# Seven products instead of eight in the second network's first layer, over 576 tokens

## The chip, the cores and the metric

The kernel runs on one core of a Trainium2 chip. The metric is the device time of one launch in microseconds (us). Between runs the time moves by about 0.2%. The core's engines run side by side, each through its own list of instructions in order: TensorE (PE; its weight loads are PEld), VectorE (DVE), ScalarE (ACT), GpSimd (POOL), and SyncE (SP), whose list holds the DMAs.

## What is computed

An attention of 4 batches, 8 heads, 576 tokens and 64 dimensions, in two parts that are added: a softmax in a window of 3 tokens to either side, and one over queries, keys and values averaged four by four. Its 2304 x 512 result goes through two networks:

```python
    a = x @ w_a            # 512 -> 1536
    b = x @ w_b
    x = a * b @ w_out      # 1536 -> 512
    h = x @ w_in           # 512 -> 2048
    g = np.maximum(h, 0.0) + alpha * np.minimum(h, 0.0)
    return (g @ w_out2)    # 2048 -> 512
```

The weights come as 64-bit floats.

## The kernel before

A matrix product in nearly fp32 is made of three fp16 ones: each operand is split into a high and a low half (`split`: ScalarE writes the scaled high half, VectorE the rest), and high x high, high x low and low x high are summed in one PSUM bank. Weights are first narrowed from 64 to 32 bits (`narrow`, three VectorE instructions), then scaled by a power of two found from the sum of their squares (`top_of`: a small fp32 transpose and matmul on TensorE between VectorE steps), then split.

The first network takes 288 tokens at a time (block j of 8): `s1(j, f)` makes 24 matmuls for one of 12 slices of hidden units and multiplies the two results, `s2(j, d)` makes 36 for one of 4 slices of the result, and `x2_out` scales, splits and writes it to DRAM. The second network takes 384 tokens at a time (6 blocks): `s3(j, f)` makes 12 matmuls of 384 columns for each of 16 slices of 128 hidden units, ScalarE takes the two halves of the leaky Relu out of the bank, VectorE joins them and the result is split into `g3`; `s4(j, t)` makes 48 matmuls of 512 columns for one of 3 tiles of 128 tokens, ScalarE scales the tile and a DMA writes it. `wi_chunk` prepares w_in, `wo2_words`, `wo2_fac` and `split_rows` prepare w_out of the second network.

No loop is issued as written. Each piece is put on a nominal time (`on`), in which order the instructions are recorded; a planner finds what each must wait for by the memory it touches, and puts every engine's list in order by a cost for each instruction (`cost`), the longest way to the end and a table of biases by name (`URGENT`). The matmuls of s1 to s4 are kept in the order of their nominal times (`chain`). `FILLS` puts matmuls of a constant tile ahead of given TensorE pieces. Since all calls go through the planner, the profile shows one line, L269, for all of them, and instructions are told apart by the tiles: `wab` and `wo` are the weights of the first network, `xt` its input, `zone` a large area that holds the attention's data first and the second network's weights later, `m`, `a` and `r` are PSUM banks (four, three and one), `tm` small buffers, `x2s` and `gt` results.

## Time and profile before

| | us |
|---|---|
| median of 3 runs (lowest, highest) | 994.26 (993.77, 995.93) |
| the profiled execution, and its span | 995.89, 994.2 |
| TensorE, VectorE, ScalarE busy in the span | 972.6, 582.8, 461.7 |
| 1152 matmuls of s3, 864 of s4, busy | 188.2, 187.6 |

The profile follows one execution. In the table a busy time is the time in which an engine had something running; matmuls overlap, so what a stream of them costs is read from the start of one group to the start of the next. The head, the first 130 us or so, holds the loads, the attention of the first batch and the first weights; then the first network runs with the other batches' attention between its matmuls, and from 615.96 us the second network.

### The profile page before, as it was taken

What the parts mean: (1) busy time and instruction counts of PE and PEld (TensorE: products, weight loads), DVE (VectorE), ACT (ScalarE), POOL (GpSimd) and SP (SyncE); (2) the same over time, 40 slices, a digit from 0 to 9 for tenths busy, and PEclk for the clock granted to TensorE, in tenths of its full rate; (3) what the DMA queues carried; (4) which work ended last, traced back from release to release, by engine and by line L of the source; (5) the groups of instructions that cost most, each with busy time, mean ns of one, the idle gap of its engine ahead of it and who ended that gap; (6) DMA issues with size and microseconds to landing.
All of it is one profiled execution on the core that took longest, in us unless ns stands there. A gap on an engine that the chain in (4) does not pass through costs nothing.

```text
span 994.2 us, 18276 instructions
## 1 busy us (share of the span) xinstructions
PE 972.6 (98%) x7443; PEld 668.4 (67%) x7443; DVE 582.8 (59%) x1270; ACT 461.7 (46%) x1123; POOL 41.1 (4%) x84
## 2 busy tenths in 40 slices
...
PEclk9998999999999999999999999999999999999999
...
GB/s 187 236 281 145 182 87 1 26 78 85 50 2 52 110 47 72 86 109 64 189 131 170 4 19 31 1 53 12 32 32 1 54 35 32 32 1 17 17 1 32
DMA packets 95940, 69.47 MB, mean 70 GB/s; under 512 B 71152, under 2 KB 78704, under 8 KB 95856
## 3 DMA queue, kind: packets, MB, share of 16 engines
...
## 4 chain that ended last, share of the span: by engine, by line
PE 88%; DVE 8%; DMA 1%; SPq 1%; ACT 1%; issue 1%; ACTq 0%
PE m L269 77%; PE a L269 9%; DVE wab L269 2%; DVE zone L269 2%; DVE wo L269 1%; PE r L269 1%; SPq L269 1%; DMA wo<-in_moe_w_b_dram 1%; DVE xt L269 1%; DMA gt<-in_v_dram 1%; DVE nm L269 1%; ACT zone L269 0%; DVE tm L269 0%; DVE gt L269 0%; DVE nz L269 0%
## 5 line engine op out<-in xcount | busy, mean ns | idle before, releaser
L269 PEld LDWEIGHTS <-wab 128*128 128x128 f16 x3168 | 306.6, 98 | 160.3 <-issue 4.1
L269 PE MATMUL m<-xt,wab 128*128 128x288 f16 x2304 | 296.0, 286 | 2.0 <-DVE xt L269 1.5
L269 PE MATMUL m<-xt,zone 128*128 128x384 f16 x1152 | 188.2, 326 | 0.0
L269 PE MATMUL m<-zone,wab 128*128 128x512 f16 x864 | 187.6, 379 | 0.0
L269 PEld LDWEIGHTS <-zone 128*128 128x128 f16 x1152 | 112.6, 98 | 74.7
L269 DVE SCALAR_TENSOR_TENSOR gt<-tm,nal,tm 128x384 f32<-128x384 f32 x96 | 59.4, 619 | 137.9 <-ACT tm L269 126.6
L269 PEld LDWEIGHTS <-wo 128*128 128x128 f16 x1152 | 111.4, 98 | 28.4 <-issue 0.6
L269 ACT ACTIVATE tm<-m 128x384 f32<-128x384 f32 (+1 forms) x224 | 95.0, 467 | 58.7 <-PE m L269 55.1
L269 PE MATMUL m<-gt,wo 128*128 128x288 f16 x864 | 109.5, 286 | 0.0
L269 DVE SCALAR_TENSOR_TENSOR wab<-gt,kap,wab 128x384 f16<-128x384 f32 x96 | 59.3, 618 | 56.6 <-ACT wab L269 56.6
L269 ACT ACTIVATE gt<-m,uf 128x512 f32<-128x512 f32 x18 | 12.4, 687 | 161.4 <-PE m L269 161.4
L269 ACT ACTIVATE wab<-gt,kap 128x384 f16<-128x384 f32 x96 | 59.0, 615 | 56.5 <-DVE gt L269 56.5
L269 PE MATMUL a<-zone 64*96 64x104 f32 (+4 forms) x1046 | 70.2, 266 | 0.0
L269 PEld LDWEIGHTS a<-zone 64*96 64x96 f32 (+4 forms) x1046 | 56.5, 149 | 18.8 <-issue 15.5
L269 ACT COPY zone<-a 104x384 f32<-104x384 f32 (+4 forms) x119 | 50.6, 470 | 31.7 <-PE a L269 31.4
L269 ACT ACTIVATE zone<-zone 128x512 bf16<-128x512 f32 (+4 forms) x48 | 39.0, 812 | 46.1 <-DVE zone L269 37.2
L269 ACT ACTIVATE gt<-tm 128x288 f16<-128x288 f32 x72 | 31.9, 442 | 51.8 <-DVE tm L269 51.4
L269 ACT COPY tm<-m 128x288 f32<-128x288 f32 x96 | 37.7, 395 | 34.5 <-PE m L269 34.2
L269 DVE SCALAR_TENSOR_TENSOR tm<-m,tm 128x288 f32<-128x288 f32 x96 | 42.7, 447 | 18.7 <-PE m L269 15.9
L269 PE MATMUL a<-idf,zone 96*104 96x96 f32 (+4 forms) x384 | 40.6, 248 | 4.3 <-DVE zone L269 4.3
L269 POOL TENSOR_TENSOR zone<-zone 72x256 f32<-72x256 f32 x36 | 32.2, 908 | 301.0 <-DMA zone<-in_v_dram 223.6
L269 DVE TENSOR_REDUCE zone<-zone 128x96 f32<-128x384 f32 x48 | 24.9, 545 | 32.6 <-ACT zone L269 32.5
...
## 6 DMA issues: line engine op xcount, KB each, us to landing
...
```

The lines of the kernel that those rows point to most:

```text
L269: f(*args, **kw)
```

## The change

Strassen's scheme in Winograd's form makes a product of 2 x 2 blocks from seven block products and fifteen additions. Here the blocks are two halves of the 512 inputs, two slices of 128 hidden units and two halves of 576 tokens. `wi_chunk` makes the seven operands of the weights (three blocks and four sums) in fp32 before the split, `x2_prep` those of the input, for which x2 is now kept in DRAM as fp32. A quarter, `s3(j, q)`, makes 14 products (`prod`, 6 matmuls of 288 columns each) for two chunks of weights side by side; each half r owns three banks (`sb3`), and sums that are needed twice stay in a bank after a copy. `done` forms the leaky Relu as max(-h, 0) x (1 - alpha) + h. The second network has 4 blocks of 576 tokens; s4 has 4 or 5 tiles after each, 18 in all. The seven operands need more room: the second network's output weights now go where the first network's `wab` was and are loaded when that comes free, and g3 goes into `wo`, `gt` and `x2s`. s1 of the last 288 tokens comes ahead of the s2 of the block before. `URGENT` and `FILLS` have new numbers throughout.

```diff
-FILLS = {0: 22, 2: 3, 9: 4, 11: 4, 17: 1, 18: 1, 19: 3, 20: 2, 28: 5, 29: 5, 30: 4, 31: 11, 35: 1, 37: 2, 38: 6,
...
+FILLS = {5: 4, 7: 1, 12: 5, 19: 2, 22: 1, 28: 2, 32: 1, 33: 1, 36: 1, 38: 5, 58: 1, 60: 34, 75: 1, 82: 1, 120: 1,
+          123: 1, 140: 2, 169: 2, 171: 1}
...
-    x2_d = [dram.tile([128, KD * 2, N1], F16, name=f"x2_d{j}") for j in range(NBL1)]
+    x2_d = [dram.tile([128, KD, N1], F32, name=f"x2_d{j}") for j in range(NBL1)]
...
-        ps = bank("r")
+        ps = bank("a" if P.name.startswith(("wi", "wo2")) else "r")
...
+    gt3 = zone[:, NZ - F1 * N1:].bitcast(F16).rearrange("p (a f n) -> p a f n", a=2, f=F1)
...
-        return gt2 if j in (1, 3) else gt
+        return gt3 if j == NBL1 - 1 else gt2 if j in (1, 3) else gt
...
-        V("tensor_tensor", out=x2_raw(d), in0=a, in1=t, op=ALU.add)
+        V("tensor_tensor", out=x2w(j)[:, d * N1:(d + 1) * N1], in0=a, in1=t, op=ALU.add)
...
-        for d in range(KD):
-            split(x2_raw(d), s, x2v[:, d, 0], x2v[:, d, 1])
-        dma(x2_d[j], x2v[:, :KD].rearrange("p d a b -> p (d a) b"))
...
+        A("activation", out=x2w(j), in_=x2w(j), func=ACTF.Copy, scale=s)
+        dma(x2_d[j].rearrange("p d n -> p (d n)"), x2w(j))
...
+    SW = 7 * 2 * 128
+
+    def wi_f(i):
+        return zone[:, i * SW:(i + 1) * SW].rearrange("p (k b n) -> p k b n", k=2, b=7)
+
+    def wi_h(i):
+        return zone[:, i * SW:(i + 1) * SW].bitcast(F16).rearrange("p (a k b n) -> p a k b n", a=2, k=2, b=7)
+
+    raws2 = [zone[:, NZ - (r + 1) * 2048:NZ - r * 2048].bitcast(I64) for r in range(4)]
+    raw2_of = [0, 1, 2, 3, 0, 1, 0, 0]
+    x2z = [zone[:, NCH * SW + n * 7 * N1:NCH * SW + (n + 1) * 7 * N1] for n in range(2)]
+    zl = zone[:, NCH * SW + 14 * N1:]
+    wabf, xtf, x2f = flat(wab).bitcast(F32), xt.rearrange("p a n -> p (a n)").bitcast(F32), x2s.bitcast(F32)
+    z2 = 2 * 2 * DM
+    wo2 = wabf[:, z2:z2 + (F2 + 1) * DM].bitcast(F16).rearrange("p (c a n) -> p c a n", a=2, n=DM)
+    raws3 = [wabf[:, :2 * DM].bitcast(I64), wabf[:, 2 * DM:4 * DM].bitcast(I64),
+             xtf[:, 7 * N1:7 * N1 + 2 * DM].bitcast(I64)]
+    raw3_of = [0, 1, 0, 1, 0, 1, 0, 1, 2, 0, 1, 2, 0, 1, 2, 0]
+    zy = z2 + (F2 + 1) * DM
...
+    GN = 2 * N1 + 64
+    gsp = [flat(wo)[:, f * 2 * GN:(f + 1) * 2 * GN] for f in range(10)]
+    gsp += [flat(gt)[:, f * 2 * GN:(f + 1) * 2 * GN] for f in range(5)] + [x2s[:, :2 * GN]]
+    g3 = [t.rearrange("p (a n) -> p a n", a=2) for t in gsp]
+    W2 = 2 * N1
+    u3s = [xt_z[0].rearrange("p a n -> p (a n)")[:, :N1], pool_f[:, :N1]]
+    cps = [[tmps[0][r][:, :N1], tmps[1][r][:, :N1], u3s[r]] for r in range(2)]
+    h1s = [zl[:, :W2], xtf[:, 7 * N1:7 * N1 + W2]]
+    h0s = [xtf[:, 7 * N1 + W2:7 * N1 + 2 * W2], zl[:, W2:2 * W2]]
+    gs = [wabf[:, r * W2:(r + 1) * W2] for r in range(3)] + [x2f[:, GN:GN + W2]]
+    obs = [x2f[:, GN + W2:GN + W2 + DM], wabf[:, zy + 7 * N1:zy + 7 * N1 + DM]]
+    sb3 = [banks["m"][:3], banks["m"][3:] + banks["a"][:2]]
+    sb4 = [banks["a"][2], banks["r"][0]]
     nal, ap_, kap = (const.tile([128, F2], F32, name=n) for n in ("nal", "alp", "kap"))
     uu = const.tile([128, 1], F32, name="uu")
...
+    def wi_words(i):
+        narrow(raws2[raw2_of[i]], wi_f(i + 1)[:, :, :4].rearrange("p k b n -> p k (b n)"), WAY[3])
+        for n in range(i + 1, NCH):
+            if raw2_of[n] == raw2_of[i]:
+                wi_load(n)
+                break
 
     def wi_chunk(c):
-        x = {}
+        m = ring("wm", [128, 2])
         for j in range(2):
-            cols_words(wi, 2 * c + j, raws2[(2 * c + j) % 4], WAY[3])
-            wi_load(2 * c + j + 4)
-        cols_bound(wi, 2 * c, x)
-        cols_split(wi, 2 * c, us_i, x)
+            wi_words(2 * c + j)
+        for j in range(2):
+            A("activation", out=zone[:, 2 * c * SW + j * 512:2 * c * SW + (j + 1) * 512].bitcast(BF16)
+              .rearrange("p (k n) -> p k n", k=2), in_=wi_f(2 * c + j + 1)[:, :, :4].rearrange("p k b n -> p k (b n)"),
+              func=ACTF.Square, accum_out=m[:, j:j + 1])
+        mr = top_of(m, 2)
+        s = ring("ws", [128, 2])
+        pow2_ss(mr, s, us_i[:, 2 * c:2 * c + 2], up=1)
+        for j in range(2):
+            w = wi_f(2 * c + j + 1)
+            for o, x, y, op in ((4, 1, 0, ALU.subtract), (0, 0, 2, ALU.add), (5, 0, 1, ALU.subtract), (6, 3, 5, ALU.subtract)):
+                V("tensor_tensor", out=w[:, :, o], in0=w[:, :, x], in1=w[:, :, y], op=op)
+            h = zone[:, (2 * c + j) * SW:(2 * c + j + 1) * SW].bitcast(F16)
+            split(zone[:, (2 * c + j + 1) * SW:(2 * c + j + 2) * SW], s[:, j:j + 1], h[:, :SW], h[:, SW:])
...
-        rows_narrow(wo2, i, F2, xr2[i % 2], WAY[4])
-        wo2_load(i + 2)
+        rows_narrow(wo2, i, F2, raws3[raw3_of[i]], WAY[4])
+        for n in range(i + 1, F2):
+            if raw3_of[n] == raw3_of[i]:
+                wo2_load(n)
+                break
...
+    def stage(j, k):
+        return xst[k if j else 0]
+
+    def x2o(j, k):
+        return (x2z[k] if j or not k else xsy).bitcast(F16).rearrange("p (a b n) -> p a b n", a=2, b=7)
+
+    def x2_load(j, k):
+        for e in range(2):
+            dma(stage(j, k)[:, 1 - e:5 - e:2], x2_d[2 * j + e][:, 2 * k:2 * k + 2])
+
+    def x2_prep(j, k):
+        x = stage(j, k)
+        for o, y, z in ((6, 2, 0), (0, 0, 1), (5, 2, 0), (4, 3, 5)):
+            V("tensor_tensor", out=x[:, o], in0=x[:, y], in1=x[:, z], op=ALU.subtract)
+        hi, lo = (x2o(j, k)[:, a].rearrange("p b n -> p (b n)") for a in range(2))
+        xf_ = x.rearrange("p b n -> p (b n)")
+        A("copy", hi, xf_)
+        V("tensor_tensor", out=lo, in0=xf_, in1=hi, op=ALU.subtract)
+
+    def prod(ps, j, c, a, b, first):
+        w = wi_h(c)
...
+            for k in range(2):
+                for x, y in ((0, 0), (0, 1), (1, 0)):
+                    T("matmul", ps[:, :N1], w[:, x, k, a], x2o(j, k)[:, y, b], start=first and n == 0, stop=(n == 5),
+                      skip_group_check=True)
                     n += 1
...
-        pos, neg = tmp(0), tmp(1)
-        A("activation", out=pos, in_=ps, func=ACTF.Relu)
-        A("activation", out=neg, in_=ps, func=ACTF.Relu, scale=-1.0)
-        g = gf[:, (f % 2) * NB:(f % 2 + 1) * NB]
-        V("scalar_tensor_tensor", out=g, in0=neg, scalar=nal[:, f:f + 1], in1=pos, op0=ALU.mult, op1=ALU.add)
-        split(g, kap[:, f:f + 1], g3[:, 0, f], g3[:, 1, f])
+
+    def s3(j, q):
+        o0 = 64 if j % 2 == 0 else 0
+        cs = (2 * q, 2 * q + 1)
+
+        def p(r, ps, a, b, first):
+            prod(sb3[r][ps], j, cs[r], a, b, first)
+
+        def keep(r, n):
+            A("copy", cps[r][n], sb3[r][0][:, :N1])
+
+        def plus(r, out, ps, n):
+            V("tensor_tensor", out=out, in0=sb3[r][ps][:, :N1], in1=cps[r][n], op=ALU.add)
+
+        def done(r, e, h):
+            f = 2 * cs[r] + e
+            g = gs[2 * r + e]
+            A("activation", out=g, in_=h, func=ACTF.Relu, scale=-1.0)
+            V("scalar_tensor_tensor", out=g, in0=g, scalar=nal[:, f:f + 1], in1=h, op0=ALU.mult, op1=ALU.add)
+            split(g, kap[:, f:f + 1], g3[f][:, 0, o0:o0 + W2], g3[f][:, 1, o0:o0 + W2])
+
+        for r in range(2):
+            p(r, 0, 1, 1, True)
+            keep(r, 0)
+        p(0, 1, 3, 3, True)
+        p(0, 0, 5, 5, False)
+        keep(0, 1)
+        p(1, 0, 5, 5, False)
+        keep(1, 1)
+        p(1, 1, 3, 3, True)
+        for r in range(2):
+            plus(r, h1s[r][:, :N1], 1, 0)
+        for r in range(2):
+            p(r, 0, 4, 6, False)
+            keep(r, 2)
+        for r in range(2):
+            p(r, 2, 0, 0, True)
+            plus(r, h0s[r][:, N1:], 2, 2)
+        for r in range(2):
+            p(r, 0, 2, 4, False)
+            A("copy", h0s[r][:, :N1], sb3[r][0][:, :N1])
+            done(r, 0, h0s[r])
+        for r in range(2):
+            p(r, 2, 6, 2, False)
+            plus(r, h1s[r][:, N1:], 2, 1)
+            done(r, 1, h1s[r])
...
+        mix = o and t == 0
+        p0 = 64 + 128 * t if not o else 512 if mix else 128 * (t - 1)
+        c = 9 * h + (t if not o else 4 + t)
+        n4[0] += 1
...
+    s2_t[NBL1 - 2], s2_t[NBL1 - 1] = tb(NBL1 - 2) + 2 * L1, tb(NBL1 - 2) + 2 * L1 + L2
+    for f in range(F1):
+        s1_t[NBL1 - 1, f] -= L2
...
+               100.0 if b == 1 else 0.0)
...
+    t2 = s2_t[NBL1 - 2]
...
-        on(t2 + 0.5 + i, lambda i=i: wo2_words(i), f"wo2w{i}", 20.0)
-        on(t2 + 18 + 0.5 * i, lambda i=i: split_rows(wo2, i, late["rf"]), f"wo2s{i}", 20.0)
-    on(t2 + 17, wo2_fac, "wo2fac", 20.0)
-    nB = tb(NBL1)
-    SB = 62.4
-    on(nB - 15, lambda: x2_load(0), "x2l0", 20.0)
...
+    L3, L4 = 41.2, 10.25
+    tt = nB
+    for j in range(4):
+        for e in range(2):
+            ti, n = (tt + 0.2, j) if j else (t2 + 0.01 * e, "0b" if e else "0a")
+            on(ti, lambda j=j, e=e: x2_load(j, e), f"x2l{n}", 20.0)
+            on(ti, lambda j=j, e=e: x2_prep(j, e), f"x2p{n}", 20.0)
+        if j:
+            tt += (4 if j % 2 else 5) * L4
+        if j % 2 == 0:
+            on(tt, lambda j=j: unscale(j // 2), f"uns{j}", 10.0)
+        for n in range(4):
+            on(tt + 0.1 + L3 / 4 * n, lambda j=j, n=n: s3(j, n), f"s3_{j}_{n}")
+        tt += L3
+        for t in range(4 + j % 2):
+            on(tt + 0.1 + L4 * t, lambda j=j, t=t: s4(j, t), f"s4_{j}_{t}")
 
```

The DMA queue, before, where the second network's output weights (`in_moe_w_out_dram` into `zone`) are loaded; they stand ahead of the first loads of x2 (`xt<-x_d`):

```order
L269 DMA zone_85<-in_moe2_w_out_dram 128x512 x2
L269 DMA xt_73<-x2_d2_79 128x8x192
L269 DMA zone_85<-in_moe2_w_out_dram 128x512 x10
L269 DMA x2_d5_82<-x2s_75 128x2304
L269 DMA zone_85<-in_moe2_w_out_dram 128x512 x2
L269 DMA xt_73<-x2_d0_77 128x8x288
L269 DMA x2_d6_83<-x2s_75 128x2304
L269 DMA xt_73<-x2_d1_78 128x8x96
L269 DMA xt_73<-x2_d1_78 128x8x192
```

And of the change, with the same weights going into `wab` and `xt`:

```order
L269 DMA zone_85<-in_moe2_w_in_dram 128x4x256 x6
L269 DMA x2_d5_82<-x2s_75 128x1152
L269 DMA wab_71<-in_moe2_w_out_dram 128x512 x8
L269 DMA xt_73<-x2_d1_78 128x2x288
L269 DMA xt_73<-x2_d0_77 128x2x288
L269 DMA xt_73<-in_moe2_w_out_dram 128x512
L269 DMA wab_71<-in_moe2_w_out_dram 128x512 x2
L269 DMA xt_73<-in_moe2_w_out_dram 128x512
L269 DMA xt_73<-x2_d1_78 128x2x288
L269 DMA xt_73<-x2_d0_77 128x2x288
L269 DMA wab_71<-in_moe2_w_out_dram 128x512 x2
L269 DMA xt_73<-in_moe2_w_out_dram 128x512
```

The sixteen loads moved from the middle of the first network's last blocks to behind the write of its sixth result, with loads of the new operand between them.

VectorE, before, from the last splits of output weights (`rf`) to the first results of s3 (`nal`, `kap`):

```order
L269 TENSOR_TENSOR x2s_75<-m0_63,tm00_86 128x288
L269 SCALAR_TENSOR_TENSOR zone_85<-zone_85,rf16_184 128x512 x3
L269 TENSOR_TENSOR x2s_75<-m2_65,tm01_87 128x288
L269 SCALAR_TENSOR_TENSOR zone_85<-zone_85,rf16_184 128x512 x2
L269 TENSOR_TENSOR x2s_75<-m0_63,tm00_86 128x288
L269 TENSOR_TENSOR x2s_75<-m2_65,tm01_87 128x288
L269 TENSOR_REDUCE xm1_159<-x2s_75 128x1
L269 SCALAR_TENSOR_TENSOR gt_74<-tm10_88,nal_114,tm00_86 128x384
L269 SCALAR_TENSOR_TENSOR wab_71<-gt_74,kap_116,wab_71 128x384
L269 SCALAR_TENSOR_TENSOR gt_74<-tm11_89,nal_114,tm01_87 128x384
L269 SCALAR_TENSOR_TENSOR wab_71<-gt_74,kap_116,wab_71 128x384
```

Of the change, from the first block of s3 on: additions from banks (`a0`, `m2`, `a1`), splits of output weights and results of s3 are mixed:

```order
L269 SCALAR_TENSOR_TENSOR uu_117<-us_o_97,us_o2_99 128x1
L269 TENSOR_TENSOR xt_73<-a0_67,tm01_87 128x288
L269 TENSOR_SCALAR uf_118<-ut_76,uu_117 128x9
L269 SCALAR_TENSOR_TENSOR wab_71<-wab_71,rf16_184 128x512
L269 TENSOR_TENSOR xt_73<-m2_65,xt0_111 128x288
L269 SCALAR_TENSOR_TENSOR wab_71<-wab_71,rf16_184 128x512
L269 TENSOR_TENSOR zone_85<-a1_68,pool_m_110 128x288
L269 SCALAR_TENSOR_TENSOR wab_71<-wab_71,rf16_184 128x512
L269 SCALAR_TENSOR_TENSOR wab_71<-wab_71,nal_114,xt_73 128x576
L269 TENSOR_TENSOR zone_85<-m2_65,tm10_88 128x288
L269 TENSOR_TENSOR xt_73<-a1_68,tm11_89 128x288
L269 SCALAR_TENSOR_TENSOR wab_71<-wab_71,rf16_184 128x512
```

The splits of the output weights moved from ahead of s3 into its first block.

TensorE, before, at the first matmuls of s3:

```order
L269 MATMUL m3_66<-gt_74,wo_72 128x288
L269 LDWEIGHTS wo_72
L269 MATMUL m2_65<-gt_74,wo_72 128x288
L269 LDWEIGHTS zone_85
L269 MATMUL m0_63<-xt_73,zone_85 128x384
L269 LDWEIGHTS zone_85
L269 MATMUL m0_63<-xt_73,zone_85 128x384
```

Of the change, ahead of the sixth product of the first block, the second step of `top_of` for the output weights, whose result is in bank a0:

```order
L269 LDWEIGHTS zone_85
L269 MATMUL m3_66<-wab_71,zone_85 128x288
L269 MATMUL a0_67<-tr1_122,ones_91 128x1
L269 MATMUL r0_70<-idf_90,xm1_159 1x128
L269 LDWEIGHTS zone_85
L269 MATMUL a0_67<-zone_85 128x288
L269 LDWEIGHTS zone_85
L269 MATMUL a0_67<-zone_85 128x288
```

That step stood within the first network before; now it is between products, in a bank that the next one takes.

## Rows read from the trace of the kernel before

**Rows 1.** Page, parts 1 and 2: busy time; granted clock in 40 slices.

```profile
PE 972.6 (98%) x7443; PEld 668.4 (67%) x7443; DVE 582.8 (59%) x1270; ACT 461.7 (46%) x1123; POOL 41.1 (4%) x84
...
PEclk9998999999999999999999999999999999999999
```

**Rows 2.** Chain of waits, longest pieces: start us, us, what ran or was waited for.

```profile
45.51 8.64 DMA wo<-in_moe_w_b_dram
...
586.62 213.76 PE m L269 x1236
```

**Rows 3.** Timeline of TensorE, end of the last s2: start us, us, what, count.

```profile
598.32 17.80 PE L269 MATMUL m<-gt,wo 128*128 128x288 f16 x144
615.96 4.23 PE L269 MATMUL m<-xt,zone 128*128 128x384 f16 x25
```

**Rows 4.** Timeline of TensorE, an s4 block, an s3 block and on.

```profile
647.16 31.24 PE L269 MATMUL m<-zone,wab 128*128 128x512 f16 x144
678.24 31.36 PE L269 MATMUL m<-xt,zone 128*128 128x384 f16 x192
709.44 10.74 PE L269 MATMUL m<-zone,wab 128*128 128x512 f16 x49
```

**Rows 5.** Instruction groups by shape, whole span: out<-in, count, busy us, mean ns.

```profile
L269 PEld LDWEIGHTS <-wab 128*128 128x128 f16 x3168 | 306.6, 98 | 160.3 <-issue 4.1
L269 PE MATMUL m<-xt,wab 128*128 128x288 f16 x2304 | 296.0, 286 | 2.0 <-DVE xt L269 1.5 <-ACT tm L269 0.3 <-DVE tm L269 0.2
...
L269 ACT COPY tm<-m 128x288 f32<-128x288 f32 x96 | 37.7, 395 | 34.5 <-PE m L269 34.2
...
L269 ACT ACTIVATE gt<-tm 128x288 f16<-128x288 f32 x72 | 31.9, 442 | 51.8 <-DVE tm L269 51.4
L269 PE MATMUL r<-warm 128*128 128x256 bf16 x187 | 29.3, 305 | 2.5 <-DVE warm L269 1.4 <-DVE ux L269 0.9 <-DVE us_ab L269 0.2
...
L269 DVE SCALAR_TENSOR_TENSOR wab<-wab,ws 128x1024 f16<-128x1024 f32 x12 | 15.3, 1276 | 2.6 <-ACT wab L269 2.6
...
L269 DVE TENSOR_TENSOR x2s<-m,tm 128x288 f32<-128x288 f32 x32 | 14.5, 452 | 29.5 <-ACT tm L269 29.1 <-PE a L269 0.4
L269 ACT ACTIVATE wab<-wab,ws 128x1024 f16<-128x1024 f32 x12 | 13.8, 1154 | 4.4 <-DVE wab L269 1.7 <-DVE ws L269 1.5 <-DVE us_ab L269 1.3
...
L269 DVE SCALAR_TENSOR_TENSOR zone<-zone,rf 128x512 f16<-128x512 f32 x16 | 12.0, 751 | 5.7 <-ACT zone L269 5.6
...
L269 ACT ACTIVATE zone<-zone,rf 128x512 f16<-128x512 f32 x16 | 11.6, 722 | 7.3 <-DVE zone L269 6.6 <-DVE us_o L269 0.5
```

**Rows 6.** Timeline of VectorE in the first network: start us, us, what.

```profile
496.32 0.45 DVE L269 TENSOR_TENSOR x2s<-m,tm 128x288 f32<-128x288 f32 x1
496.68 1.27 DVE L269 SCALAR_TENSOR_TENSOR zone<-zone,ws 128x1024 f16<-128x1024 f32 x1
497.88 0.68 DVE L269 SCALAR_TENSOR_TENSOR zone<-zone 128x512 uint32<-128x512 uint32 x1
```

**Rows 7.** Timeline of ScalarE in an s3 block.

```profile
639.86 0.85 ACT L269 ACTIVATE tm<-m 128x384 f32<-128x384 f32 x2
```

**Rows 8.** Busy time by stretch: PE, PEld, DVE, ACT, POOL; clock, DMA, GB/s.

```profile
500.00:550.00 50.00, 50.00 (x409) 39.81 (x408) 37.45 (x85) 23.08 (x60) 0.00 (x0) 1.00 0.44 141
...
650.00:700.00 50.00, 50.00 (x266) 25.88 (x265) 12.23 (x20) 15.97 (x34) 0.00 (x0) 1.00 0.08 27
```

**Rows 9.** Timeline of the DMA queue while second output weights load.

```profile
497.23 33.41 SPq L269 DMA_DIRECT2D zone<-in_moe_w_out_dram  x10
```

**Rows 10.** Busy time by stretch in the head, columns as in rows 8.

```profile
75.00:80.00 5.00, 5.00 (x42) 3.86 (x42) 3.97 (x10) 2.38 (x10) 2.12 (x3) 0.51 0.66 215
...
90.00:95.00 5.00, 3.45 (x37) 2.58 (x38) 5.00 (x11) 4.64 (x17) 2.41 (x3) 1.00 0.41 58
```

More of the change, by code (lines that the diff above doesn't have):

```diff
@@ L102, in cost @@
             st = list(ins[0].ap)
-            half = int(st[0][1]) <= 64 or self.free(ins[0]) <= 64
-            return max(n / (1200 if half else 600) + 0.002, 0.13 if int(st[0][1]) > 2 else 0.3), 0.2
+            half = 800 if int(st[0][1]) <= 64 else 1200 if self.free(ins[0]) <= 64 else 600
+            return max(n / half + 0.002, 0.13 if int(st[0][1]) > 2 else 0.3), 0.2
         m = max([n] + [self.free(a) for a in ins])
@@ L365 @@
     NB = 384
-    NBLK = NT // NB
     N1 = S // 2
@@ L585 @@
     one = [const.tile([3 * H, HALF], BF16, name=f"one{h}") for h in range(H)]
-    pool_m = const.tile([WK, 3, 120], F32, name="pool_m")
+    pool_f = const.tile([128, 360], F32, name="pool_m")
+    pool_m = pool_f[:WK].rearrange("p (a n) -> p a n", a=3)
     LR = 3 * H * D
@@ L1131, in s3, with unscale @@
-    def s3(j, f):
-        x2 = x2_of(j).rearrange("p (d a) n -> p d a n", a=2)
-        ch, e = divmod(f, FPC)
-        ps = bank("m")[:, :NB]
+        V("scalar_tensor_tensor", out=uu, in0=us_o, scalar=2.0 ** (81 + sum(WAY)), in1=us_o2, op0=ALU.mult, op1=ALU.mult)
+    def unscale(h):
+        V("tensor_scalar_mul", uf[:, 9 * h:9 * h + 9], ut[:, 9 * h:9 * h + 9], uu)
+    def stage(j, k):
+        return xst[k if j else 0]
+    def x2o(j, k):
+        return (x2z[k] if j or not k else xsy).bitcast(F16).rearrange("p (a b n) -> p a b n", a=2, b=7)
@@ L1135, in s3 @@
+    def prod(ps, j, c, a, b, first):
+        w = wi_h(c)
         with pe(True):
             n = 0
-            for kk in range(KD):
-                wh = wi[:, ch, 0, kk, e * 128:(e + 1) * 128]
-                wl = wi[:, ch, 1, kk, e * 128:(e + 1) * 128]
-                for a, bb in ((wh, x2[:, kk, 0]), (wh, x2[:, kk, 1]), (wl, x2[:, kk, 0])):
-                    T("matmul", ps, a, bb, start=(n == 0), stop=(n == 3 * KD - 1))
-                    n += 1
-        pos, neg = tmp(0), tmp(1)
-        A("activation", out=pos, in_=ps, func=ACTF.Relu)
```

124 lines of the change are left out of this document (54 added, 70 removed), and 48 rows, old and new, of the table URGENT.

## The prediction

> **What bounds the kernel now.** I read four views, from the coarse to the fine. The page's first part and the granted clock come first: TensorE is busy for 972.6 of 994.2 us, and the clock granted to it is 8 tenths in one early slice and 9 or more in all others [rows 1]. A busy share alone proves little, so the chain of waits is second: from 586.62 us on its pieces are TensorE's matmuls and hardly anything else, the first of them 213.76 us long; before about 130 us it also runs through VectorE and a DMA [rows 2]. So the second network, where the change is, is limited by TensorE and by nothing else, and the first 130 us by something else. Third comes the timeline of TensorE. It gives what a matmul costs in a stream: 144 matmuls of 288 columns stand from 598.32 to 615.96 us, 0.1225 us each, although they alternate between two banks [rows 3]. One block of first products of the second network (192 of 384 columns) takes 678.24 to 709.44 = 31.20 us, 0.1625 each, and one block of second products (144 of 512 columns) 647.16 to 678.24 = 31.08 us, 0.2158 each [rows 4]. Last come the busy times by stretch: in the second network VectorE works 12.23 and ScalarE 15.97 of 50 us; in the last blocks of the first network, while words are narrowed, VectorE works 37.45 of 50 [rows 8]. TensorE is the scarce engine, and the others have room; the question is whether the change uses up that room.
>
> The sum is made against the profiled execution, 995.89 us (its span 994.2 and 1.69 around it). The median of the three runs shown is 994.26, 1.63 lower; I carry that over at the end.
>
> **Step 1: the products, -22.6 us.** Before: 6 blocks x 31.20 = 187.2 us. After: a quarter of s3 has 14 products of 6 matmuls with 288 columns, 84 x 0.1225 = 10.29 us; four quarters make 41.2 us for 576 tokens, and 16 quarters 1344 x 0.1225 = 164.6 us. The matmul form is that of [rows 3], so I use its rate. The second products stay 18 x 48 = 864 of 512 columns. All of it is on the path that sets the end, so 187.2 - 164.6 = 22.6 us go. A bound on the rate is the block itself: at no better than 0.1225 and no worse than the 0.1625 of [rows 4], a gain of 22.6 or a loss of 31; I take 0.1225, since the very shape is measured with banks alternating.
>
> **Step 2: emptying the banks in s3, +1 us (0 to +8).** This is the price of Strassen's scheme. In a quarter ScalarE makes 8 copies out of PSUM with 288 elements (0.395 us), 4 Relu from SBUF with 576 and 4 scaled conversions with 576. The last two were not in the trace; from 0.442 at 288, and 0.722 and 1.154 at 512 and 1024 (0.00084 per element) I work out 0.68 and 0.78. Sum 3.16 + 2.72 + 3.12 = 9.0 us. VectorE makes 6 additions from PSUM (0.452) and 8 scalar_tensor_tensor with 576: 0.751 + 64 x 0.00103 = 0.82, the slope from 0.751 and 1.276. Sum 2.71 + 6.56 = 9.3 us [rows 5]. That is 90% of TensorE's 10.29. But durations overlap: on VectorE independent instructions start 0.07 to 0.09 us before the one ahead ends [rows 6], on ScalarE two of 0.477 take 0.85 [rows 7]. With 14 x 0.08 and 16 x 0.1 off, VectorE needs 8.2 and ScalarE 7.4 us of 10.29. Before, a stall in s3 was excluded by room; now the room is 20%. A bank is written again two products (1.47 us) after its last matmul at the earliest; emptying it takes 0.286 for that matmul to land and 0.395 for the copy, so an instruction of 0.78 may be ahead of the copy and just fits. Hence near nothing per quarter, 0.06 x 16 = 1 us; the bound above is 0.5 per quarter.
>
> **Step 3: the second weights late, +3 us (0 to +14).** Words: a row costs VectorE one instruction of 0.42 and two of 0.69 (1.8 us), and a load; before, ten loads were issued in 33.41 us without hurry, 3.3 us each [rows 9]. Now 16 loads must follow each other through two, later three buffers, from when s1 has used its first two of twelve weight slices for the last 288 tokens to the end of s2. 16 x 3.3 = 53 us, and there are 29 (ten twelfths of s1's 35.3) and 35 (two s2 of 17.64). VectorE in those last 35.3 us before s3: eight rows of words 14.3, two preparations of the new operand 8.1 (four subtractions of 288 and one of 2016 each), eight s2 results 3.6, two maxima 2.7 and some 30 small ones of 0.15: 33 us, less the overlap 30. It fits, barely; s2's banks come free by these instructions, so a late load is late matmuls. I take +1, from 0 to +8.
>
> The 16 splits then fall into the first s3 block: 16 x 0.751 on VectorE and 16 x 0.722 on ScalarE. VectorE has 4 x 9.3 + 12.0 = 49.2 us to do there against TensorE's 41.2. The order shows only three splits before the first quarter ends, since the row factors need two small TensorE steps first; by about 11.2 us VectorE is through ten of these rows, and 63 rows of 43.0 us are left, 38.0 with the overlap. It ends at 49.2 us. TensorE needs the last of them when it reaches the fourth group of the first s4 tile: 41.2 + 36 x 0.2158 = 49.0 us. That is late by nothing to speak of; for waits between the two engines, which alternate on each split, I take +2, from 0 to +6. The Trainium skill, VectorE: DVE Perf Modes, section "The DRAIN you can't avoid", says that the next VectorE instruction starts only when the one before has left the pipeline, with an exception for some pairs that have no wait between them. By it the 43.0 us would stand in full, the end would be at 54.2 and the loss 5.2 us; here instructions do start before the end of the one before, by 0.07 to 0.09 [rows 6], so I keep that as an upper end.
>
> **Step 4: the scale of the second weights, +0.6 us (0 to +1).** Their bound now goes through bank a0, which is also the bank of the sixth product of s3. The small fp32 step stands right ahead of that product, VectorE must read its result, and behind it TensorE waits in order. A landing (0.27) and a read (0.15) with the handing over make about 0.6, once.
>
> **Step 5: what is hidden, 0.** Each later x2 block is loaded and prepared under s4: 8.1 us of VectorE and 3.8 of ScalarE in 41 to 43 us of TensorE, where these two otherwise only empty a tile each 10.3 us. Loads for the second block queue behind each other on the DMA queue and behind one output, some 20 us of work in 41. The eight column chunks of first weights need 55 instead of 35 us of VectorE (6.9 a chunk, with four more subtractions and a split over 1792 instead of 1024 elements), in the blocks of s1 and s2 that come before; but the rows of second weights, 16 x 2.6 = 41 us, leave that stretch, where VectorE was busy 37.45 of 50 us with them [rows 8]. If that cover failed, s1 would wait for VectorE, 5 us at the most by these two numbers.
>
> **Step 6: the head, 0 (-5 to +6).** 67 filler matmuls instead of 193 (187 in the trace, 29.3 us [rows 5]). Most of them fill time in which TensorE waits for VectorE, which is busy 5.00 of 5 us from 90 to 95 us [rows 10]. The 34 that stay ahead of the dense s1 keep their place. VectorE's work ahead of the third s1 pair and of the twenty-fourth is the same within 2 us by the order. Behind a stretch in which TensorE waited, the granted clock was near the lower of its two levels (0.51 in 75 to 80 us [rows 10]); fewer fillers may lengthen such stretches. Against it, a load of w_b that was the longest wait of the chain there, 8.64 us [rows 2], now stands ahead of six loads.
>
> **Sum.** -22.6 + 1 + 1 + 2 + 0.6 = -18.0; 995.89 - 18.0 = 977.9, and 1.63 less for the median: **976 us**.
>
> **Rivals.**
> A, late weights starve the matmuls (0.15): the upper ends of step 3. For it: VectorE has 30 of 35 us full and every load waits for a row of words. Against it: loads took only 3.3 us. 976 + 10 = 986.
> B, slower (0.08): s3 is bound by emptying banks, not by TensorE. Both engines take work strictly in order; if two instructions of 0.78 stand ahead of a copy, the bank is 0.286 + 0.395 + 1.56 = 2.24 us away against 1.47, TensorE waits 0.77. There are four such places in a quarter. At half of them that is 1.5 a quarter and 24 us in all: 976 + 24 - 1 = 999. It decides from 18.0 / 16 = 1.1 us a quarter. For it: nothing of the kind ran before; against it: 20% of room.
> C, the products save no time since more and shorter matmuls cost as much each (0.02): 1344 against 1152. Both rates are in the rows, so it needs weight loads that hold the stream up, and these take 98 ns, below 122 [rows 5]. At 0.139 for 288 columns the gain is gone: 998. The Trainium skill, TensorE: Matmul & The Clock Gate, section "Back-to-back issue gap", gives streams of weight loads and matmuls 81 ns at 128 columns and 131 ns at 512. Straight between these an estimate is 102 and 114 ns, 1344 x 0.102 against 1152 x 0.114, and the change would cost 6 us; the trace has 122 and 162 (and 216 at 512), and the measurement decides.
> D, better (0.12): nothing of steps 2 to 4 shows and the head gains 2 to 3: 970.
>
> **How the numbers follow.** My forecast, 971 to 982, has 0.60; A 0.15, B 0.08, C 0.02, D 0.12, and 0.03 is for losses that just eat the gain. A measurement of this kernel can tell 0.2%, 2 us, from no change: faster is below 992.3. Faster: 0.60 + 0.15 + 0.12 = 0.87; same 0.03; slower 0.08 + 0.02 = 0.10. The range takes in the forecast and most of A and D: 968 to 988.
>
> **What would show it.** Step 1: a steady quarter of s3 takes 10.3 us on TensorE, with matmuls 0.1225 apart. Step 2: VectorE busy some 80 to 90% in s3 blocks two to four, with no idle time of TensorE ahead of the m banks. Step 3: idle time of TensorE, if any, around the end of s2 and in the first block or its first s4 tile, which is longer than the later ones by 2 to 6 us. Step 4: one wait for a0. I am wrong if quarters of the later blocks take over 11 us (B), if matmuls stand over 0.13 apart (C), or if the dense s1 begins much after 95 us (step 6).

## The result: 970.7 us, and the profile after

The changed kernel takes 970.69 us (median of 4 runs, 969.37 to 971.35); the kernel before took 994.35 us (4 runs) beside it. The ratio is 0.9758, with an interval of 0.9741 to 0.9775. The forecast was 976 (968 to 988). The profiled execution of the changed kernel took 971.35 us with a span of 969.5, 24.7 us less than the 994.2 of the kernel before.

The page of the changed kernel, to be held against [rows 1]; the letters are tenths of 40 slices of the span:

```profile
PE 938.7 (97%) x7515; PEld 678.0 (70%) x7515; DVE 633.7 (65%) x1341; ACT 469.3 (48%) x1075; POOL 44.0 (5%) x84
...
DVE  5999997676567765536898888796278008606700
...
PEclk9978999999999999999999999999999999999999
```

The VectorE line of the kernel before, in slices of nearly the same length:

```profile
DVE  5999988576666766777977485613406144061340
```

TensorE is still busy for 97% of a shorter span. The granted clock is now below 9 tenths in two early slices. In the last fifteen slices, about those of the second network, VectorE had 6 tenths at the most in an s3 block; now the slices of the later s3 blocks have 7 8, 8 6 and 6 7.

TensorE's timeline around the first two s3 blocks (start and length in us, operands, count, and in brackets how long it waited for what):

```profile
606.09 4.58 PE L269 MATMUL m<-zone,wo 128*128 128x288 f16 x36
610.51 0.53 PE L269 MATMUL m<-zone 128*128 128x288 f16 x3
...
655.24 0.53 PE L269 MATMUL a<-wab,zone 128*128 128x288 f16 x3 [2.54 <-DMA wab<-x_d]
...
697.04 3.84 PE L269 MATMUL m<-zone 128*128 128x288 f16 x30
707.33 3.84 PE L269 MATMUL m<-zone 128*128 128x288 f16 x30
...
738.20 6.64 PE L269 MATMUL r<-wab,wo 128*128 128x512 f16 x30
...
748.56 6.64 PE L269 MATMUL a<-wab,wo 128*128 128x512 f16 x30
```

The s2 ends at 610.51 us, where [rows 3] had 615.96. The second s3 block stands from 697.04 to 738.20: 41.16 us, its quarters 10.29 apart (697.04, 707.33). The third and the fourth take 41.16 too. The s4 tiles are 10.36 us apart (738.20, 748.56), as before (31.08 for three, [rows 4]). The first block ends right behind the row at 655.24: three matmuls are 0.37 us, so s4 starts at 655.61 and the block took 45.10. Of the 3.94 us more, 2.54 are the wait in that row; the other 1.40 are mostly the small steps for two scales, which stand between products (0.71 us for the first, see step 4 below; 0.40 at 642.2).

TensorE's waits, summed by what was waited for (us, times, the longest), as far as a sum is over 0.6 us:

```profile
PE a L269 <- DVE zone L269: 15.1, 4, 9.1
PE m L269 <- POOL one L269: 3.9, 1, 3.9
PE a L269 <- DMA wab<-x_d: 2.5, 1, 2.5
PE r L269 <- DVE td L269: 1.3, 2, 0.9
PE m L269 <- DVE wab L269: 1.3, 1, 1.3
PE m L269 <- ACT zone L269: 0.9, 2, 0.7
PE m L269 <- DVE tm L269: 0.7, 1, 0.7
```

Only the third line is behind 150 us. So the account by place is: everything ahead of s3 5.45 us shorter, s3 18.6 shorter (187.2 to 3 x 41.16 + 45.10 = 168.6), s4 the same; 24.1 of the 24.7 us between the spans.

### The profile page after: what moved, and what is told of

It is laid out like the page before. It is cut to its first block, busy times and chain, and to the rows that moved or that the text cites. A ratio compares the mean times of both kernels' runs of the same rounds, so it can differ in the third digit from the quotient of the medians.

```text
span 969.5 us, 18422 instructions
## 1 busy us (share of the span) xinstructions
PE 938.7 (97%) x7515; PEld 678.0 (70%) x7515; DVE 633.7 (65%) x1341; ACT 469.3 (48%) x1075; POOL 44.0 (5%) x84
## 3 DMA queue, kind: packets, MB, share of 16 engines
q1 hardware_dynamic: 87760, 68.31, 25.9%
## 4 chain that ended last, share of the span: by engine, by line
PE 87%; DVE 7%; DMA 2%; ACT 2%; SPq 1%; issue 1%; ACTq 0%
PE m L269 54%; PE a L269 23%; PE r L269 10%; DVE wab L269 2%; DVE zone L269 1%; SPq L269 1%; DVE wo L269 1%; DMA x2s<-in_moe_w_out_dram 1%; ACT zone L269 1%; DMA zone<-in_v_dram 1%; DVE xt L269 1%; DMA zone<-in_k_dram 0%; DVE nm L269 0%; ACT gt L269 0%; DVE tm L269 0%
## 5 line engine op out<-in xcount | busy, mean ns | idle before, releaser
L269 PEld LDWEIGHTS <-wab 128*128 128x128 f16 x2304 | 222.5, 98 | 60.7 <-issue 2.7
L269 PEld LDWEIGHTS <-wo 128*128 128x128 f16 x1692 | 164.1, 98 | 91.4 <-issue 0.6
L269 PE MATMUL m<-zone 128*128 128x288 f16 (+3 forms) x982 | 132.2, 285 | 0.0
L269 PE MATMUL a<-zone 64*96 64x104 f32 (+5 forms) x1298 | 110.4, 274 | 0.0
L269 ACT COPY tm<-m 128x288 f32<-128x288 f32 x160 | 61.7, 394 | 49.1 <-PE m L269 48.8
L269 DVE SCALAR_TENSOR_TENSOR tm<-m,tm 128x288 f32<-128x288 f32 x96 | 43.1, 451 | 31.3 <-PE m L269 25.9
L269 PE MATMUL a<-wab,wo 128*128 128x512 f16 x270 | 59.7, 379 | 0.0
L269 PE MATMUL r<-wab,wo 128*128 128x512 f16 x270 | 59.7, 379 | 0.0
L269 PE MATMUL m<-zone,wo 128*128 128x288 f16 x432 | 55.6, 286 | 0.0
L269 PEld LDWEIGHTS a<-idf,zone 96*104 96x104 f32 (+4 forms) x384 | 35.3, 135 | 19.8 <-ACT zone L269 9.4
L269 PEld LDWEIGHTS <-gt 128*128 128x128 f16 x270 | 26.4, 98 | 31.9
```

What stands on the lines that cost most here:

```text
L269: f(*args, **kw)
```

## The experiments

All were timed beside the kernel before, and ratios are to it. The spans compared below are those of profiled executions.

**The wait at the end of the first s3 block.** The last product reads two slices of its operand in `wab` (high and low half, bytes 1152 to 1727 and 5184 to 5759 of a row); one of the two loads of the next block's x2 into that area writes bytes 0 to 1151 and 2304 to 3455. They touch nothing in common, and the planner, which keeps such strided areas apart, saw no conflict and put this load ahead of the product. The wait was added when the program was built from that order. These are the two instructions in the order of the changed kernel, with what each waits for:

```
119 L269 DMA wab_71<-x2_d3_80 128x2x288 [waits PE_49]
8542 L269 MATMUL a1_68<-wab_71,zone_85 128x288 [waits DMAHW0_49]
```

The product waits for a DMA. The experiment `e1_no_wait` only puts that load behind the other one, which must follow the product:

```diff
             dma(stage(j, k)[:, 1 - e:5 - e:2], x2_d[2 * j + e][:, 2 * k:2 * k + 2])
+        if (j, k) == (1, 1):
+            P.ops[-1].preds.add(P.ops[-2])
```

> Edit: the second of the two x2 loads that go into the wab tile for block 1 is made to follow the first, which has to follow the last product of s3's first block anyway. Theory (that product waits for a load that it has nothing to do with: the load writes other bytes of the same tile, and was put ahead of it in the order): the wait of 2.54 us at 655.24 us goes and nothing takes its place, first s3 block 42.6 instead of 45.1 us, 968.2 us (970.7 - 2.5). Rival (the wait only covers VectorE and ScalarE, which are behind there with the splits): TensorE waits in the first s4 tile instead, which takes over 12 instead of 10.36 us, 970 to 971.

Measured: 968.1 us, ratio 0.9738 (0.9723 to 0.9754); span 966.5, 3.0 less. The two loads on SyncE, in the changed kernel and then in this one, from the timelines:

```profile
652.37 3.80 SPq L269 DMA_DIRECT2D wab<-x_d  x2
```

```profile
652.78 0.89 SPq L269 DMA_DIRECT2D wab<-x_d  x2
```

The 3.80 us are no transfer: the first load was issued at 652.37, and the second had to wait for the product, which waited for the first. Now s4 starts at 652.59, 42.40 us behind the start of s3 at 610.19, and its first tile is 10.36 us long (the next begins at 662.95). The theory holds: the wait is gone and nothing takes its place. The intervals of the two ratios overlap; it is the trace that tells the difference.

**Emptying the banks.** `e7_drain2` and `e8_drain4` compute low halves twice, for half of the results (with `if r:` ahead of it) or for all:

```diff
             split(g, kap[:, f:f + 1], g3[f][:, 0, o0:o0 + W2], g3[f][:, 1, o0:o0 + W2])
+            V("scalar_tensor_tensor", out=g3[f][:, 1, o0:o0 + W2], in0=g, scalar=kap[:, f:f + 1],
+              in1=g3[f][:, 0, o0:o0 + W2], op0=ALU.mult, op1=ALU.subtract)
```

> Edit: in s3, half of the results have their low half computed twice (two more VectorE instructions of 0.81 us a quarter, 0.73 each with the overlap). VectorE then needs 8.30 + 1.46 = 9.76 of 10.29 us a quarter. Theory (only the sum counts, since the banks are copied out first): steady quarters stay at 10.29 us, the first block, where VectorE also splits the second weights, takes 0 to 3 us more, 970.5 to 974. Rival B (the order in front of the bank copies counts): 0.3 to 1.1 us a quarter, 976 to 988.

> Edit: in s3 every result has its low half computed twice (four more VectorE instructions a quarter). VectorE then needs 8.30 + 2.92 = 11.2 of 10.29 us a quarter. Theory: s3 is bound by VectorE, quarters of the later blocks go to 11.2 us after the first one or two of a block, the first block, with the splits, to some 53 us; 8 for that and 3 x 2.7 for the others, 984 to 990. Rival (VectorE lags into s4, where it has time, and the banks do not wait for it): under 976.

Measured: 973.53 us (ratio 0.9807, 0.9788 to 0.9826) and 984.49 us (0.9913, 0.9895 to 0.9931). A steady quarter of the changed kernel, of `e7_drain2` and of `e8_drain4` (stretch, its length, then busy time and count of PE, PEld, DVE, ACT and POOL, clock, DMA share and GB/s):

```profile
707.33:717.62 10.29, 10.29 (x86) 8.22 (x84) 8.30 (x15) 7.84 (x17) 0.00 (x0) 1.00 0.01 2
```

```profile
708.90:719.19 10.29, 10.29 (x86) 8.20 (x84) 9.57 (x17) 7.84 (x17) 0.00 (x0) 1.00 0.01 2
```

```profile
725.87:736.16 10.29, 10.29 (x86) 8.20 (x84) 10.29 (x19) 7.88 (x17) 0.00 (x0) 1.00 0.01 2
```

VectorE goes from 8.30 to 9.57 and to all of 10.29 us, and TensorE does not lose a hundredth of a us. What VectorE does not get done is late in s4. The first s4 tile of `e8_drain4`:

```profile
655.23 6.64 PE L269 MATMUL r<-wab,wo 128*128 128x512 f16 x30
661.70 1.46 PE L269 MATMUL r<-wab,gt 128*128 128x512 f16 x6
664.84 0.60 PE L269 MATMUL r<-wab,gt 128*128 128x512 f16 x2 [1.68 <-ACT gt L269]
669.75 3.35 PE L269 MATMUL r<-wab,gt 128*128 128x512 f16 x7 [4.30 <-DVE gt L269]
672.88 1.49 PE L269 MATMUL r<-wab,x2s 128*128 128x512 f16 x3
674.16 1.07 PE L269 MATMUL a<-wab,wo 128*128 128x512 f16 x4
```

This tile takes 18.93 us, 8.57 too long, and the first tile of the second block, for instance, 11.63 (746.45 to 758.08), 1.27 too long. 8.57 and three times 1.27 make 12.4 us; s3 began 0.3 earlier, and the span grew by 12.0. In `e7_drain2` the first tile takes 11.67 us and that of the second block 10.40. My theory had the times about right and the place wrong: the quarters and the first block do not grow at all. Rival B is refuted for VectorE over a block of four quarters: the work queued there does not hold the banks, but the results that s4 reads. Three limits of this should be kept in mind. VectorE's list takes the additions from banks ahead of the splits that are queued. A block starts with VectorE idle (for 12.55 us ahead of the second block of `e8_drain4`), so what is queued grows for four quarters and no longer. And no run put more work on ScalarE, busy for 7.84 of 10.29 us, whose copies come first in emptying the banks; that side is untested.

**The order.** `e4_old_numbers` gives the changed kernel both old tables; `e5_late_old` gives it the old biases only for the names alphas, wi, wo2, x2 and uns; `e6_before_new_numbers` gives the kernel before the new tables, cost and release:

```diff
-FILLS = {5: 4, 7: 1, ...}
-URGENT = {"": 145, "alphas": 60, ...}
+FILLS = {0: 22, 2: 3, ...}
+URGENT = {"alphas": -10, "b0@0": 10, ...}
...
-URGENT = {... "wi0": 30, "wo2s": 165, "wo2w": 60, "x2_0": 85, ...}
+URGENT = {... "wi0": 200, "wo2s": 115, "wo2w": -80, "x2_0": 110, ...}
...
-            half = int(st[0][1]) <= 64 or self.free(ins[0]) <= 64
+            half = 800 if int(st[0][1]) <= 64 else 1200 if self.free(ins[0]) <= 64 else 600
```

> Edit: both tables of numbers (biases and fillers) as before, the rest as changed; names that only the changed kernel has get no bias. Theory (the 5.45 us that the first network gained are the new order's): s3 begins at about 616 us, and the time is 975 to 980, more if s3's first block waits without its biases. Rival (the gain comes with the code: the preparation of x2 and of the second weights left that stretch): s3 begins within 1 us of 610.5, 970 to 972.

> Edit: of the biases only those of the second network's preparation (alphas, the first weights wi, the second weights wo2, x2 and uns) as in the kernel before, all others and the fillers as changed. Theory (with all old numbers s3 began some 35 us later, most of it since VectorE could no longer fit the late weights and the first weights in, rival A of the prediction): s3 begins 12 to 25 us later than 610.5 us, TensorE waits 10 us or more for VectorE between 550 and 650 us, 983 to 996 us. Rival (the 35 us come from the first network's biases, which let VectorE fall behind from the head on): s3 begins within 4 us of 610.5, 970 to 975.

> Edit: the kernel before (eight products) with both new tables, the new cost of fp32 matmuls and the later release of the sums of v, as far as its names are the same. Theory (the head's gain is the new order's and has nothing to do with Strassen's scheme): s3 begins 3 to 6 us earlier than 615.96, 988 to 992 us. Rival (the tables fit only the code they stand in): no gain, 994 or more, with new waits in the second network.

Measured: 1009.05 us (ratio 1.0169, 1.0145 to 1.0192), 1000.74 (1.0076, 1.0059 to 1.0093) and 1007.43 (1.0141, 1.0122 to 1.0160). The second goes the theory's way, somewhat past its upper end; the first lost far more than I expected, and the third went the rival's way. TensorE in `e5_late_old`, at the end of s2:

```profile
593.47 1.63 PE L269 MATMUL m<-gt,wo 128*128 128x288 f16 x12 [3.06 <-DVE x2s L269]
...
615.07 0.38 PE L269 MATMUL r<-tr,ones 1*128 1x1 f32 x2 [3.17 <-DVE tr L269]
625.33 11.15 PE L269 MATMUL m<-zone,wo 128*128 128x288 f16 x72 [9.89 <-DVE xt L269]
636.43 0.53 PE L269 MATMUL m<-zone 128*128 128x288 f16 x3
```

and the stretch ahead of the last row but one:

```profile
600.00:625.00 25.00, 12.28 (x100) 9.67 (x98) 24.33 (x50) 13.91 (x22) 0.00 (x0) 0.82 0.53 174
```

VectorE is busy for 24.33 of 25 us, TensorE for 12.28. s3 begins at 636.43, 25.9 us late, and the span is 27.3 longer. Of the 25.9 us, 6.3 are lost before the last two s2, which begin at 581.02 instead of 574.71, and 19.6 in them: they take 55.41 us instead of 35.80, with waits of 16.1 us in these rows. That is rival A in part. The late weights do starve s2 if VectorE takes them in a worse order; but in 581 to 625 us VectorE also makes four splits of w_in, of 2.08 us each, which the changed kernel has done by 561, and the run doesn't tell these from the late output weights. With all old numbers s3 begins at 645.37, 34.9 us late, so these few names would be most of it, if such effects add.

The new numbers in the old kernel show the other half. Its dense s1 begins at 86.28 us, as in the changed kernel (86.04; before, 94.75), and it has done 398 matmuls of s1 by 150 us, against 386 and 367. These are the groups of `e6_before_new_numbers`, of the changed kernel and of the kernel before, from 0 to 150 us (count, then busy us and mean ns, then idle time by what ended it):

```profile
L269 PE MATMUL m<-xt,wab 128*128 128x288 f16 x398 | 54.0, 291 | 2.3 <-DVE wab L269 1.3 <-DVE tm L269 0.7 <-ACT tm L269 0.4
```

```profile
L269 PE MATMUL m<-xt,wab 128*128 128x288 f16 x386 | 52.7, 292 | 2.0 <-DVE wab L269 1.3 <-DVE tm L269 0.7
```

```profile
L269 PE MATMUL m<-xt,wab 128*128 128x288 f16 x367 | 48.2, 286 | 2.0 <-DVE xt L269 1.5 <-ACT tm L269 0.3 <-DVE tm L269 0.2
```

The 31 matmuls that are done earlier are worth (398 - 367) x 0.1225 = 3.8 us. These are the first long piece of s1 in the kernel before, the changed kernel, `e6_before_new_numbers` and `e3_old_fills` (the changed kernel with the fillers of the kernel before, see below):

```profile
94.75 5.92 PE L269 MATMUL m<-xt,wab 128*128 128x288 f16 x47 [1.49 <-DVE xt L269]
```

```profile
86.04 7.82 PE L269 MATMUL m<-xt,wab 128*128 128x288 f16 x60
```

```profile
86.28 7.67 PE L269 MATMUL m<-xt,wab 128*128 128x288 f16 x60
```

```profile
92.61 7.81 PE L269 MATMUL m<-xt,wab 128*128 128x288 f16 x60
```

So the gain in the head comes with the new numbers and not with Strassen's scheme. The fillers are needed for it: with the old ones most of it is gone. `e6_before_new_numbers` changes biases, fillers, cost and release at once and doesn't say what each of them gives.

The new numbers spoil that kernel's 500 to 600 us, where TensorE stands idle for 10.7 of 100, and its s3 begins at 627.94. Each set of numbers fits the code that it was made for, and with the old set the change as a whole is a loss (1.0169).

Where Strassen's own gain lies can be read from the same four spans. From the start of s3 to the end it is 378.2 us in the kernel before (994.2 - 616.0) and 378.2 with the new numbers (1006.1 - 627.9), but 359.0 in the changed kernel (969.5 - 610.5) and 361.6 with the old numbers (1007.0 - 645.4). The gain of the second network holds with either set; what the numbers move lies almost all ahead of s3.

**The fillers.** `e2_no_fills` has none, `e3_old_fills` the 193 of the kernel before (187 in the trace):

```diff
-FILLS = {5: 4, 7: 1, ...}
+FILLS = {}
```

> Edit: no filler matmuls at all (67 in the changed kernel). Theory (in the head TensorE waits for VectorE, so that the fillers only lie in gaps and keep the clock up): without them the granted clock is near its lower level in more of the first 90 us, dense s1 begins 1 to 3 us later, 971.7 to 973.7. Rival (the fillers themselves hold TensorE up: 34 of them, some 4.2 us, stand ahead of one piece near 60 us): dense s1 begins earlier, 967 to 970.

> Edit: the 193 fillers of the kernel before at their places, all else as changed. Theory (the head's gain of about 4 us is due to the new order of VectorE's work, fillers lie in gaps): within 1 us of the changed kernel, 970 to 972. Rival (the gain is that of 18 us of fillers that no longer stand ahead of pieces): s3 begins 3 to 5 us later, 974 to 976.

Measured: 974.48 us (ratio 0.9802, 0.9781 to 0.9823) and 975.47 (0.9811, 0.9792 to 0.9831): both worse than with 67. Two stretches of `e2_no_fills`, and the same two of the changed kernel:

```profile
40.00:50.00 10.00, 10.00 (x85) 8.40 (x84) 7.64 (x16) 4.93 (x11) 0.00 (x0) 0.52 1.10 225
50.00:60.00 10.00, 2.16 (x24) 2.00 (x23) 9.28 (x25) 6.55 (x24) 0.00 (x0) 0.67 0.99 342
```

```profile
40.00:50.00 10.00, 5.34 (x82) 4.45 (x82) 10.00 (x25) 5.68 (x23) 0.00 (x0) 0.96 1.11 206
50.00:60.00 10.00, 5.47 (x42) 4.21 (x42) 8.59 (x22) 6.09 (x13) 0.00 (x0) 0.50 1.03 387
...
80.00:90.00 10.00, 10.00 (x76) 7.57 (x75) 8.71 (x15) 6.47 (x24) 0.00 (x0) 0.67 0.33 64
```

Without fillers about the same number of matmuls fill all of 40 to 50 us, at a granted clock of 0.52 (near 1.2 GHz) instead of 0.96 (near 2.4), and s3 begins at 614.03, 3.5 us late. With the old ones s3 begins at 616.31, 5.8 us late, so my theory that fillers only lie in gaps was wrong there: the piece of TensorE that began at 54.40 us begins at 57.15, behind fillers and still after a wait of 3.62 us for VectorE.

The last two rows of the changed kernel also show where it still loses. TensorE waits 9.06 us up to 54.40, and then works at the lower level; it does so again behind the wait of 4.18 us that ends at 79.43. `e9_fill_early` and `e10_fill_late` put more fillers into one of these gaps, `e11_fill_both` into both, all with the load moved as in `e1_no_wait`:

```diff
-FILLS = {..., 58: 1, 60: 34, ...}
+FILLS = {..., 50: 44, 58: 1, 60: 64, ...}
```

> Edit: the load moved as in the first experiment (968.1 us), and 44 fillers ahead of the piece that begins at 54.40 us, where TensorE had stood idle for 9.06 us and the granted clock then was 0.50 from 50 to 60 us. Theory (the idle time costs the clock of the work behind it, and that work is on the chain): the 5.6 us from 54.40 to 60.01 and the first s1 slice, 2.93 us, run at the upper level, dense s1 and s3 begin 2 to 4 us earlier, 964 to 966 us. Rival (VectorE sets the pace of the head, a sooner TensorE piece only waits for it): 967.5 to 969. Against both: fillers that last longer than the idle time, over 969.

> Edit: the load moved, and 64 instead of 34 fillers at 71 us, ahead of the piece at 79.43 us for which TensorE waited 4.18 us; the granted clock was 0.67 from 80 to 90 us. Theory (as for the early place): the 6.6 us from 79.43 to 86.04 us shrink to some 4, 965 to 966.5 us. Rival (VectorE sets the pace): 967.5 to 969.

> Edit: the load moved, 44 fillers at the early and 64 at the late place. Theory: the two gains add, 961 to 964 us. Rival (VectorE sets the pace): 967.5 to 969.

Measured: 967.45 us (ratio 0.9733, 0.9720 to 0.9746), 967.09 (0.9725, 0.9712 to 0.9739) and 964.83 (0.9711, 0.9698 to 0.9725). Singly, the times are just below the rival's and cannot be told from 968.1. Together they give 3.3 us, half of what the theory made of them; by the ratios, since the two were not timed beside each other, it is 2.7, and the intervals just touch. In the traces s3 begins 3.7 us before that of `e1_no_wait` (606.47 for 610.19), and singly 1.56 and 0.15 before it. In `e10_fill_late` the filled gap did bring s1 forward (84.04 us for 86.04), but the granted clock was 0.86 in 120 to 130 us, where `e1_no_wait` has 1.00, and 12 matmuls there took 3.04 us instead of 1.63. From the timeline and the stretches of `e11_fill_both`:

```profile
47.30 6.63 PE L269 MATMUL r<-warm 128*128 128x256 bf16 x44 [2.21 <-DVE ux L269]
54.14 0.84 PE L269 MATMUL a<-idf,zone 96*104 96x96 f32 x8 [0.21 <-DVE zone L269]
55.22 0.72 PE L269 MATMUL a<-mask,idb 96*96 96x416 bf16 x2 [0.24 <-ACT zone L269]
57.57 1.64 PE L269 MATMUL m<-xt,wab 128*128 128x288 f16 x12
59.16 4.88 PE L269 MATMUL m<-xt,wab 128*128 128x288 f16 x36
65.92 0.87 PE L269 MATMUL a<-idf,zone 96*104 96x96 f32 x8 [1.78 <-DVE zone L269]
```

```profile
50.00:60.00 10.00, 9.37 (x90) 6.99 (x88) 9.74 (x24) 7.83 (x21) 0.00 (x0) 0.93 1.04 384
...
80.00:90.00 10.00, 9.28 (x82) 7.10 (x83) 10.00 (x20) 7.77 (x29) 0.00 (x0) 1.00 0.51 109
```

The clock is up (0.93 for 0.50, 1.00 for 0.67), and from the piece at 54 us to the second pair of s1 it takes 5.0 us instead of 8.5 (54.40 to 62.94). Then the piece at 65.92 waits 1.78 us for VectorE, so over half is given back: 3.78 us ahead at the second pair (59.16 for 62.94), 1.54 ahead at this piece (65.92 for 67.46). s3 begins at 606.47, 4.0 us before the changed kernel. This is the best version tried: 964.8 us, with the whole interval of its ratio below that of the changed kernel.

**The scale of the second weights.** `e12_top_r` takes step 4 back:

```diff
-        ps = bank("a" if P.name.startswith(("wi", "wo2")) else "r")
+        ps = bank("r")
```

> Edit: the scale of the second network's weights again through the bank r instead of a. Theory (step 4 of the prediction, 0.6 us for one wait at a0): first s3 block 0.3 to 0.6 us shorter, the time within 1 us of the changed kernel, 970 to 971. Rival (bank r is also the bank of the fillers and of the first s4 tile, and of x2's scale, so that the small steps wait for each other there): 971 to 974.

Measured: 974.72 us (ratio 0.9807, 0.9793 to 0.9820). TensorE at the end of s2 and the start of s3:

```profile
601.37 4.77 PE L269 MATMUL m<-zone,wo 128*128 128x288 f16 x24 [2.28 <-DVE xt L269]
...
614.78 0.53 PE L269 MATMUL m<-zone 128*128 128x288 f16 x3 [0.98 <-ACT tm L269]
```

The rival has the direction, and the time is past its upper end. s2 waits 2.28 us for VectorE and s3's first quarter 0.98, s3 begins 2.4 us late, and the first block is not shorter (612.90 to 658.32, 45.4 us, or 44.4 without the 0.98). Why it was so, the shared bank or only another order that follows from it, this run does not separate.

## Why the prediction was right, and where not

The sign, the mechanism and the largest term were right; the time came out 5.3 us below, in the range, but just under the 971 to 982 that I held likely, at rival D's 970. Step by step:

**Step 1, -22.6.** Measured -22.6: 4 x 41.16 = 164.6 against 187.2, with matmuls 0.1225 us apart, the rate of [rows 3]. Rival C is out. On its rule in the Trainium skill, TensorE: Matmul & The Clock Gate, section "Back-to-back issue gap": the estimates of 0.102 and 0.114 us that I worked out from it for 288 and 384 columns do not occur here, neither before nor after; 0.1225 and 0.1625 do, and the measurement decides.

**Step 2, +1 (0 to +8).** Measured 0. The load was estimated well (VectorE 8.30 and ScalarE 7.84 of 10.29 us, against 8.2 and 7.4), the consequence was not. I took 80% to be near a limit of the banks; `e8_drain4` shows that with VectorE at 100% the banks still come free in time, for four quarters; more load on ScalarE was not tried. The price of a full VectorE is the start of s4. The steady quarter also answers the rule in the Trainium skill, VectorE: DVE Perf Modes, section "The DRAIN you can't avoid": in full the durations would make 9.3 us a quarter, and the trace has 8.30.

**Step 3, +3 (0 to +14).** Measured 0. The trace lists no wait of TensorE between 150 and 655 us, and the first s4 tile is as long as the others. But the doubt was right in kind. The cover is thin, as "It fits, barely" said: in 575 to 600 us VectorE is busy for 23.98 of 25. In `e5_late_old`, where other work of the second network falls into the same stretch, the last two s2 take 19.6 us longer. That is beyond the 14 that I allowed; several waits of s2 for a full VectorE follow one another there.

**Step 4, +0.6.** Measured 0.71. The slot of the product before ends at 614.30, the small step's matmul runs at 614.39, VectorE reads its result from 614.80 to 614.96, and the product that takes a0 starts at 615.01. The second small step, at 642.2, took 0.40 more, which the sum had not priced. Undoing step 4 did not give this back but cost 4 us.

**Step 5, 0.** Nothing showed of the later loads, preparations and chunks, except the one thing that I had not looked for: a load of the next block's x2 that is issued early, and the last product of the block waiting for it (2.54 us). I asked what each load waits for, and not what waits for the load.

**Step 6, 0 (-5 to +6).** This step was off by the most, and just beyond its lower end. Everything ahead of s3 became 5.45 us shorter. Some 4 us are of the head. TensorE's busy time from 150 us to the start of s3 is 460.2 us against 464.5 before, since 19 more matmuls of s1, and more of the attention, are done by then. The rest is a wait of 1.25 us for ScalarE at 333 us that is gone. I had argued that VectorE's order ahead of s1 was the same within 2 us and let fillers count for nothing. They count both ways: 187 of them cost 4.8 us, none 3.8, against these 67, and with the 187 the whole 5.45 is gone (s3 at 616.31).

The errors: steps 2 and 3 were 4 us too dear and step 6 left out 5.45; against it, 2.54 us of wait and some 0.7 of small steps in the first block were not foreseen. That is some 6.2 of the 6.5 us by which the profiled executions (24.5 us apart) passed the sum's 18.0; the rest is within the noise. That the time fell on rival D's 970 is partly luck: the gain ahead of s3 (5.45) and the loss in the first block (3.94) nearly cancel, and I had foreseen neither.
